# A one-core mixer kernel: means added to the transposed activations one step sooner, and query features of tiles 10 to 15 transposed by VectorE through DRAM instead of by TensorE

## The chip, the cores and the metric

The kernel runs on one core of one Trainium2 chip. The metric is the device time of one execution in microseconds (us). Three timed executions of the kernel before gave 625.36, 626.11 and 626.40 us: median 626.11 us. All arithmetic is float32; a product of two matrices is made of three passes on TensorE (high part by high part, high by low, low by high; lines 54 to 58), since TensorE takes its operands in a rounded form of float32.

## The reference

With x of shape 2048 x 512, the output is x plus two branches that both read the layer-normalised x. Cut to what matters:

```
xn = layernorm(x)
# branch A: linear attention, 32 heads of 16
q, k, v = split(xn @ wqkv)
phi(t)  = concat(softmax(t_head @ w_phi), softmax(-t_head @ w_phi))   # 32 features a head
kv = sum over rows of phi(k)^T v ;  z = sum over rows of phi(k)
A  = (phi(q) @ kv) / (phi(q) . z + 1e-6) @ wo
# branch B: gated MLP that mixes rows
zz = gelu(xn @ w_in);  z1, z2 = halves of zz (688 columns each)
B  = (z1 * (w_sp @ layernorm(z2) + b_sp)) @ w_out
out = x + A + B
```

## The kernel before

The 2048 rows are 16 tiles of 128 (numbered 0 to 15). Five stages follow each other, and TensorE (PE) runs the matrix products of all of them one after the other.

1. **Projections** (lines 485 to 518, up to about 205 us in the profile). The loop runs over steps s = 0 to 15. Each step makes the features of the keys of tile s (`proj_k`), the values of the next tile (`proj_v`), and, run a bit faster so that 16 are made in 13 steps, the query features (`proj_q`), which go unnormalised to DRAM in `e_d`, by a DMA on GpSimd's (POOL's) queue. In between stand pieces of `z1_raw`, the half z1 of branch B, whose matmuls read as `zps`.
   Tiles 6 to 15 of x come already transposed from DRAM (`lay_x`, tile `xc` or `xt`). Their row means are not subtracted on an engine: `send_mean(s+4)` computes the means of tile s+4 (VectorE; a sign change on POOL, line 311; SyncE (SP) stores them to DRAM in `nm_d`, line 312), and `center_t` issues, on POOL's queue, a DMA that reads the means from `nm_d` as a broadcast and adds them to `xc` as it lands (line 318). `split_x(s+2)` then makes the two parts of `xT` (ScalarE, line 48; VectorE, line 52), which TensorE multiplies in the next step. In step s the call was `center_t(s+3)`: the tile whose means had been sent a step before, and whose `xT` is made one step later.
   The running sum of the key features is made by accumulating DMAs on POOL's queue too (`zacc`, line 342).
2. **The second half of branch B's input** (`zproj` with `w2`, gelu, layer norm), up to about 290 us.
3. **The row mixing** w_sp @ z2 in seven products of a Strassen form (`products`, matmuls `g`), up to about 490 us.
4. **Output** (lines 1016 to 1044), up to the end. It goes over pairs of tiles i = 0, 2, ... 14. In program order TensorE does for a pair: `project_u(i)` (15 + 2 matmuls of branch B's output product), `attend` (32 small matmuls `po` of query features by kv), `project_u(i+1)`, `project_o(i)`, `project_o(i+1)` (12 matmuls each, adding branch A's output product), and then `attend_T(i+2)`: 16 transposes on TensorE (`ptq`, line 936) of the next pair's query features, which ScalarE copies to `f` (line 938). `po` of the next pair reads `f`.
   The query features come back from `e_d` (`load_q`, tile `et`, SP's queue). `features(s)`, three tiles ahead of the pair's loop, normalises them with seven VectorE instructions (`q_fin`, lines 542 to 549) and a DMA on POOL's queue copies them to a rounded tile `er` (line 905), which the transposes read. VectorE also makes the low parts of `u` and of `oT` (`ul`, `oT`, line 52), which `project_u` and `project_o` read.
   The last rows of branch B's gate are still made in this stage (`gate` at i = 8, lines 785 to 798): a VectorE transpose in blocks of 32 x 32 (line 795), four stores on SP's queue to `u_d`, and loads of `u` from there for tiles 14 and 15 (line 813). The same way of turning a tile, over DRAM in four stores of one block each, had been used for all other tiles before.
   Output tiles go out by accumulating DMAs on POOL's queue (`out<-xr`, line 984); `xr` has three buffers, the PSUM tile `out` two.

Instructions of an engine run in the order in which they stand in its program, and the DMAs of SP and of POOL are issued in that order too: one that waits holds up all behind it. That order is made from the code by a scheduler with estimated times, within the bounds that `tc.issue_after` sets. `xz_tile`/`slot` is a ring of 16 buffers shared by `et`, `qtmp` and others; a buffer is given out again when its readers are done.

Of the kernel before, what the change touches and what calls it, by code (L numbers as in the profile page):

```python
# [10 lines left out]
F32 = mybir.dt.float32  # L11
# [7 lines left out]
P = 128  # L19
S, D, H, DH, FH = 2048, 512, 32, 16, 688  # L20
NT = S // P
ND = D // P
FC = FH // 2
NG = 4
NF = 2 * D
# [3 lines left out]
BL = 32  # L29
EPS_LN = 1e-5  # L30
EPS_DEN = 1e-6
XB = 5
FT, LT = 6, 13
NP = NT // 2
HP, QP = P // 2, P // 4
FP = 3 * P
# [4 lines left out]
def mixer(ctx: ExitStack, tc: tile.TileContext, x, x_t, wv, wqkT, phi_bd, wo, w_in, wst, b_r, w_out, out):  # L41
    nc = tc.nc
    pe, act, dve, pool, sp = nc.tensor, nc.scalar, nc.vector, nc.gpsimd, nc.sync
# [34 lines left out]
    u_d = dram.tile([NT, FU, P], F32, name="u_d")  # L78
    kvT_d = dram.tile([P, D], F32, name="kvT_d")
    zb_d = dram.tile([P, NF], F32, name="zb_d")  # L80
    nm_d = dram.tile([NT, ND, P], F32, name="nm_d")

    ident = cst.tile([P, P], F32, name="ident")
# [13 lines left out]
    def heads(ap):  # L97
        return ap.rearrange("p (h d) -> p h d", d=DH)
# [8 lines left out]
    def bc(ap, n):  # L107
        return ap.unsqueeze(2).to_broadcast([P, n, DH])
# [66 lines left out]
    with ExitStack() as p0:  # L175
# [138 lines left out]

        def center_t(s):

            with tc.issue_after(send_mean.last):
                pool.dma_start(lay[s], nm_d[s].rearrange("c t -> (c t)").unsqueeze(0).to_broadcast([P, D]), accum_op=ALU.add)

        def keep_v(s, p):  # L320
# [12 lines left out]

        def proj_q(s):
            e = softmax_pair(wk, proj(s, wqk_h[:, 0], wqk_l[:, 0]), "q", r_x[:, s:s + 1])
            pool.dma_start(e_d[s], e)

        def add_kv(s, er):

# [142 lines left out]
        keep(pe=zproj.last)  # L482
        spare.update(zip((2, 3, 4, 5, 8, 9), [bd_t] + wkT_t + wqT_t[:1] + [None] * 2))
        n1, nq = 1, 0
        for s in range(NT):
            if s + 4 < FT:
                fetch(s + 4)
            if FT <= s + 6 < NT:
                fetch(s + 6)
            if FT <= s + 4 < NT:  # L490
                lay_x(s + 4)
            er = ek[s] if s < len(ek) else proj_k(s)
            if 1 < s < FT - 2:
                centered(s + 2)
            elif FT - 2 <= s < NT - 2:
                with tc.issue_after(softmax_pair.last[0]), tc.issue_after(softmax_pair.last[1]):
                    split_x(lay.pop(s + 2))
            if FT <= s + 4 < NT:
                send_mean(s + 4)
            if FT <= s + 3 < NT:  # L500
                center_t(s + 3)
            while nq < (s - 2) * NT // (NT - 3):
                proj_q(nq)
                nq += 1
            add_kv(s, er)
            if s == 0:
                tiles = fold_tiles(((za, "z"), (ps, "mm")))
                keep(pe=fold(0, wqT, tiles))
                folded(0, tiles)
            elif s == 1:  # L510
                proj_v(3)
            elif 2 < s < NT - 1:
                proj_v(s + 1)
            while n1 < s * (NT - LAG) // (NT - 1):
                z1_raw(wk, za, n1, 2)
                n1 += 1
            if s == 3:
                queue.close()
# [19 lines left out]
    def q_fin(et, tmp, zb):  # L538

        e, r, t, w = et[:, :NF], *(et[:, NF + k * 2 * H:NF + (k + 1) * 2 * H] for k in range(3))  # L540
        den = et[:, NF + 6 * H:QW]
        dve.tensor_tensor(tmp, e, zb, op=ALU.mult)
        dve.tensor_reduce(t, heads(tmp), axis=AX.X, op=ALU.add)
        dve.tensor_tensor(t, t, r, op=ALU.mult)
        dve.scalar_tensor_tensor(den, pairs(t, 0), EPS_DEN, pairs(t, 1), op0=ALU.add, op1=ALU.add)
        dve.reciprocal(den, den)
        dve.tensor_tensor(w.rearrange("p (h a) -> p h a", a=2), r.rearrange("p (h a) -> p h a", a=2),
                          den.unsqueeze(2).to_broadcast([P, H, 2]), op=ALU.mult)
        return e, dve.tensor_tensor(heads(e), heads(e), bc(w, 2 * H), op=ALU.mult).ins

    QC = 4
    NQ = NT // QC
# [249 lines left out]
    def slot(name, dt=F32):  # L802
        return xz_tile(2 * FH, dt, name)
# [92 lines left out]

    def features(s):
        with tc.issue_after(fin[-1]):
            es[s], ins = q_fin(ets.pop(s), slot("qtmp")[:, :NF], zb)
        fin.append(ins)  # L900
        if s == 3:
            return
        e = es[s]
        es[s] = cw.tile([P, NF], F32R, tag="er", bufs=6, name="er")
        lasts[6] = pool.dma_start(es[s].bitcast(F32), e).ins
# [19 lines left out]
    def attend_T(s):  # L925

        fs = []
        for g in range(NG):
            pt = pst.tile([P, 2, 2, P], F32, tag="tr", name="ptq")
            for a in range(2):  # L930
                for k in range(2):
                    src = group(es[s + k], 2 * g + a)
                    if src.dtype == F32:
                        pe.transpose(pt[:, a, k], src, ident)
                    else:
                        pe.transpose(pt[:, a, k].bitcast(F32R), src, ident_r)  # L936
            f = wk.tile([P, 2, 2 * P], F32, tag="f", bufs=NG + 1, name="f")
            lasts[5] = act.activation(f, pt.rearrange("p a k b -> p a (k b)"), AF.Copy).ins
            fs.append(f)
        return fs  # L940
# [137 lines left out]
```

## Time and profile before

| | |
|---|---|
| median of three timed runs | 626.11 us |
| the profiled execution, its time | 625.34 us |
| its span, first to last instruction | 623.6 us |
| granted TensorE clock, mean | 0.999 |
| VectorE (DVE) busy | 508.3 us (82%) |
| ScalarE (ACT) busy | 272.8 us (44%) |
| GpSimd (POOL) busy | 113.7 us (18%) |
| DMA moved | 103.67 MB, mean 166 GB/s |

The rows quoted below come from the page of the profiled execution (engines, chain of the work that ended last, DMA issues) and from answers of its trace: waits by engine, timelines by engine (start in us, length in us, engine, line, operation, output <- input, shape, and in brackets the idle time before and what ended it), and windows (busy us of each engine in a stretch, number of instructions, granted clock, DMA share, GB/s). A matmul's length there is longer than the step to the next one, since matmuls are pipelined: what counts is from start to start. For a DMA the trace shows the issue on its queue, and "us to landing" is counted from there.

### The profile page before, as it was taken

Reading aid. Unit: us, or ns where it says so; the run is one execution under the profiler, and the core shown is the slowest. Engines: PE = TensorE matmul, PEld = TensorE weight load, DVE = VectorE, ACT = ScalarE, POOL = GpSimd, SP = SyncE. Lnnn points to the kernel's source line nnn. Section 1 sums busy time; section 2 is a strip of 40 time slices with the busy share of each in tenths; the row PEclk is TensorE's granted clock in tenths of the full one; section 3 lists DMA queues with packets and bytes.
Section 4 is the critical chain, followed back from the end, with each engine's and each line's share of the span. In section 5 each row is a group of like instructions: output and inputs, shape, how many; then the busy total and the mean of one; then the engine's idle time right before and its main releaser. Section 6 shows DMA issues by size and latency. Waiting matters only on the chain.

```text
span 623.6 us, 11439 instructions
## 1 busy us (share of the span) xinstructions
PE 615.1 (99%) x4366; PEld 561.5 (90%) x4366; DVE 508.3 (82%) x903; ACT 272.8 (44%) x436; POOL 113.7 (18%) x198
## 2 busy tenths in 40 slices
PE   8999999999999999999999999999999999999997
PEld 7888888878889999999999999999999887788785
DVE  5999899899988498988989888696959899989211
ACT  4652324333433558876435433253444433334331
POOL 4122233222211025541000000000000212211110
PEclk9999999999999999999999999999999999999999
DMA  9557676566546757002464745637477799984722
GB/s 318 189 138 165 162 183 187 152 165 172 118 154 186 271 210 270 2 1 67 129 128 136 196 89 155 156 97 173 88 177 244 225 284 332 328 243 111 162 38 48
DMA packets 90671, 103.67 MB, mean 166 GB/s; under 512 B 47080, under 2 KB 60136, under 8 KB 90376
## 3 DMA queue, kind: packets, MB, share of 16 engines
q1 hardware_dynamic: 76840, 60.76, 34.0%
q0 software_dynamic: 11472, 36.54, 23.6%
q10 hardware_dynamic: 2304, 5.64, 2.4%
q8 instruction: 34, 0.56, 0.4%
q14 instruction: 21, 0.17, 0.1%
HBM read 61.61 MB, written 30.56 MB: 148 GB/s over the span
## 4 chain that ended last, share of the span: by engine, by line
PE 85%; DMA 6%; DVE 4%; issue 3%; POOL 1%; ACT 1%; DVEq 0%; POOLq 0%
PE g L58 11%; PE g L57 10%; PE g L56 10%; PE zps L58 6%; PE zps L56 6%; PE zps L57 6%; PE pout L56 5%; PE pout L58 5%; PE pout L57 5%; DMA xc<-nm_d 5%; PE proj L56 4%; PE proj L57 4%; PE proj L58 4%; PE ptq L936 1%; PE po L951 1%
## 5 line engine op out<-in xcount | busy, mean ns | idle before, releaser
L57 PE MATMUL g<-B,A 128*128 128x344 f32 x448 | 143.4, 320 | 0.0
L56 PE MATMUL g<-B,A 128*128 128x344 f32 x448 | 142.9, 320 | 0.0
L58 PE MATMUL g<-B,A 128*128 128x344 f32 x448 | 140.7, 321 | 0.1
L56 PEld LDWEIGHTS g<-B,A 128*128 128x128 f32 x448 | 84.3, 188 | 0.0
L57 PEld LDWEIGHTS g<-B,A 128*128 128x128 f32 x448 | 84.2, 188 | 0.0
L58 PEld LDWEIGHTS g<-B,A 128*128 128x128 f32 x448 | 83.7, 188 | 0.4 <-DVE A L52 0.4
L48 ACT ACTIVATE A<-S 128x512 fp32r<-128x512 f32 x64 | 39.2, 629 | 76.3 <-DVE S L588 61.3
L121 ACT ACTIVATE e<-e,r_x 128x1024 f32<-128x1024 f32 x26 | 29.9, 1150 | 56.3 <-DVE e L120 55.1
L56 PE MATMUL proj<-wqk_h,xT 128*128 128x512 f32 x128 | 50.1, 391 | 0.0
L57 PE MATMUL proj<-wqk_l,xT 128*128 128x512 f32 x128 | 50.0, 390 | 0.0
L58 PE MATMUL proj<-wqk_h,xT 128*128 128x512 f32 x128 | 49.9, 390 | 0.0
L48 ACT ACTIVATE A<-wf 128x512 fp32r<-128x512 f32 (+1 forms) x64 | 33.1, 519 | 33.3 <-DMA wf<-in_wst 12.6
L52 DVE TENSOR_TENSOR A<-S,A 128x512 fp32r<-128x512 f32 x64 | 43.0, 686 | 4.4 <-ACT A L48 4.0
L56 PE MATMUL zps<-w_0h,xT 128*128 128x344 f32 x128 | 41.1, 321 | 0.0
L56 PE MATMUL zps<-w_1h,xT 128*128 128x344 f32 x128 | 40.9, 319 | 0.0
L58 PE MATMUL zps<-w_0h,xT 128*128 128x344 f32 x128 | 40.8, 319 | 0.0
L58 PE MATMUL zps<-w_1h,xT 128*128 128x344 f32 x128 | 40.7, 319 | 0.0
L57 PE MATMUL zps<-w_1l,xT 128*128 128x344 f32 x128 | 40.6, 318 | 0.0
L57 PE MATMUL zps<-w_0l,xT 128*128 128x344 f32 x128 | 40.6, 318 | 0.0
L753 POOL DMA_DIRECT2D z1t<-z_d x16 | 8.6, 545 | 166.9 <-DMA u_d<-z1t 124.9
L52 DVE TENSOR_TENSOR A<-wf,A 128x512 fp32r<-128x512 f32 (+1 forms) x64 | 35.0, 549 | 1.8 <-ACT A L48 1.8
L124 DVE TENSOR_REDUCE sm<-e 128x64 f32<-128x1024 f32 x26 | 31.2, 1200 | 1.7 <-ACT e L121 1.5
(218 smaller groups left out, 1430.6 us busy)
## 6 DMA issues: line engine op xcount, KB each, us to landing
wf<-in_wst SPq DMA_DIRECT2D x64, 256.0 KB, 3.1
e_d<-e POOLq DMA_DIRECT2D x16, 544.0 KB, 5.0
et<-e_d SPq DMA_DIRECT2D x16, 544.0 KB, 5.2
er<-et POOLq DMA_DIRECT2D x12, 512.0 KB, 5.5
z_d<-z1f ACTq DMA_DIRECT2D x16, 344.0 KB, 2.3
z1t<-z_d POOLq DMA_DIRECT2D x16, 344.0 KB, 5.3
zacc<-e POOLq DMA_DIRECT2D x10, 512.0 KB, 4.7
u<-u_d SPq DMA_DIRECT2D x15, 320.0 KB, 6.3
```

What stands on the lines that cost most here:

```text
L48: return act.activation(h, src, AF.Copy).ins
L52: return (eng or dve).tensor_tensor(l, src, h.bitcast(F32), op=ALU.subtract).ins
L56: pe.matmul(dst, ah, bh, start=start, stop=False)
L57: pe.matmul(dst, ah, bl, start=False, stop=False)
L58: return pe.matmul(dst, al, bh, start=False, stop=stop).ins
L121: softmax_pair.last = less, act.activation(e, e, AF.Exp, scale=scale).ins
L124: dve.tensor_reduce(sm, heads(e), axis=AX.X, op=ALU.add)
L753: pool.dma_start(t[:, k, :FH], z1_d[2 * i + k])
L936: pe.transpose(pt[:, a, k].bitcast(F32R), src, ident_r)
L951: lasts[3] = pe.matmul(po[r][c * QP:(c + 1) * QP, k], kvT[rows, m // 2, cols], fs[m // 4][rows, m // 2 % 2], start=True, stop=True).ins
```

## The change

Two things are changed. First, in stage 1 step s calls `center_t(s + 4)` in place of `center_t(s + 3)`, behind `proj_q` in place of ahead of it, and the DMA is put behind the last `e_d` store in POOL's order. So the means of a tile are added in the step that sends them. Second, from tile TQ = 10 on, `features(s)` transposes the normalised features with VectorE (`turn_q`: 128 x 1024 in blocks of 32 x 32, into the tile `qtmp`), stores them in four DMAs on POOL's queue to a new DRAM tensor `q_d` in runs of 32 elements (128 bytes), and drops the copy to `er`; `attend_T` of the pairs 10, 12 and 14 is then four loads of `f` on SP's queue (`load_f`, 256 KB each, in runs of 1 KB), with no TensorE transpose and no ScalarE copy. The diff, cut:

```diff
+TQ = 10
...
+    q_d = dram.tile([NP, NF, 2, P], F32, name="q_d")
...
         def center_t(s):
-            with tc.issue_after(send_mean.last):
+            with tc.issue_after(send_mean.last), tc.issue_after(proj_q.last or send_mean.last):
                 pool.dma_start(lay[s], nm_d[s].rearrange("c t -> (c t)").unsqueeze(0).to_broadcast([P, D]), accum_op=ALU.add)
...
         def proj_q(s):
...
-            pool.dma_start(e_d[s], e)
+            proj_q.last = pool.dma_start(e_d[s], e).ins
...
             if FT <= s + 4 < NT:
                 send_mean(s + 4)
-            if FT <= s + 3 < NT:
-                center_t(s + 3)
             while nq < (s - 2) * NT // (NT - 3):
                 proj_q(nq)
                 nq += 1
+            if FT <= s + 4 < NT:
+                center_t(s + 4)
             add_kv(s, er)
...
+    def turn_q(s, dst, e, eng=sp):
+        ins = dve.transpose(dst, e).ins
+        q = q_d[s // 2, :, s % 2].rearrange("(m j) t -> j m t", j=BL)
+        for b in range(0, P, BL):
+            turn_q.last = eng.dma_start(q[:, :, b:b + BL], dst[b:b + BL].rearrange("p (m t) -> p m t", t=BL)).ins
+        return ins
+
+    def load_f(s, f, g):
+        sp.dma_start(f, q_d[s // 2, 2 * g * P:2 * (g + 1) * P].rearrange("(a p) k t -> p a (k t)", p=P))
+        return f
...
     def features(s):
         with tc.issue_after(fin[-1]):
-            es[s], ins = q_fin(ets.pop(s), slot("qtmp")[:, :NF], zb)
+            tmp = slot("qtmp")[:, :NF]
+            es[s], ins = q_fin(ets.pop(s), tmp, zb)
+            if s >= TQ:
+                ins = turn_q(s, tmp, es.pop(s), pool)
         fin.append(ins)
+        if s >= TQ:
+            return
...
     def attend_T(s):
         fs = []
+        if s >= TQ:
+            return [load_f(s, wk.tile([P, 2, 2 * P], F32, tag="f", bufs=NG + 1, name="f"), g) for g in range(NG)]
```

The lines of the new program are numbered 1 to 22 higher, so line 52 reads as 53, 318 as 320, 549 as 552, and 798 as 813. How the order moves, at three places:

On POOL, in a step of stage 1, the program before reads (`mask` holds the means that line 311 turns in sign, `xc<-nm_d` is the adding DMA of `center_t`, and the brackets name what an instruction waits for: DMAHW is a DMA of SP or ScalarE, DMASW one of POOL):

```order
L311 TENSOR_SCALAR mask<-mask 128x32 [waits DVE_49]
L94 TENSOR_SCALAR mask<-mask 128x1
L318 DMA xc<-nm_d 128x512 [waits DMAHW3_49,DMAHW0_49]
L95 TENSOR_TENSOR r_x<-mask,mhalf 128x1 [waits Pool_49]
L342 DMA zacc<-e 128x1024 [waits DMASW1_49,DMASW4_49,DVE_49,Activation_49]
L336 DMA e_d<-e 128x1088 [waits DMASW5_49,DVE_49,Activation_49]
```

and now:

```order
L313 TENSOR_SCALAR mask<-mask 128x32 [waits DVE_49]
L96 TENSOR_SCALAR mask<-mask 128x1
L97 TENSOR_TENSOR r_x<-mask,mhalf 128x1 [waits Pool_49]
L320 DMA xc<-nm_d 128x512 [waits DMAHW5_49,DMAHW4_49]
L344 DMA zacc<-e 128x1024 [waits DMASW2_49,DMASW5_49,DVE_49,Activation_49]
L338 DMA e_d<-e 128x1088 [waits DMASW6_49,DVE_49,Activation_49]
```

The place is nearly the same, between the sign change and `zacc`; the tile is another: the DMA now waits for the store of the means that the sign change just ahead of it has released.

On PE, where pair 8 ends and pair 10 begins (`woh` is the high part of wo, `wu` of w_out), the program before reads:

```order
L58 MATMUL pout<-woh,oT 128x512
L936 MATMUL ptq<-zb,er 128x128 [waits DMASW2_49,PE_49]
L936 MATMUL ptq<-zb,er 128x128 [waits DMASW3_49]
L936 MATMUL ptq<-zb,er 128x128 x2
L936 MATMUL ptq<-zb,er 128x128 [waits PE_49]
L936 MATMUL ptq<-zb,er 128x128 x3
L936 MATMUL ptq<-zb,er 128x128 [waits PE_49]
L936 MATMUL ptq<-zb,er 128x128 x3
L936 MATMUL ptq<-zb,er 128x128 [waits PE_49]
L936 MATMUL ptq<-zb,er 128x128 x3
L56 MATMUL pout<-wu,uh 128x512 [waits Activation_49]
```

and now:

```order
L57 MATMUL pout<-woh,oT 128x512
L58 MATMUL pout<-wol,oT 128x512
L59 MATMUL pout<-woh,oT 128x512
L57 MATMUL pout<-wu,uh 128x512 [waits Activation_49]
L58 MATMUL pout<-wu,uh 128x512
L59 MATMUL pout<-wu,ul 128x512
```

The 16 transposes are gone between the last matmul of `project_o(9)` and the first of `project_u(10)`, and so they are for pairs 12 and 14. Where `po` of these pairs waited for ScalarE's copy, it now waits for the loads of `f`.

On VectorE and SP in the last part of the program, VectorE before reads, from the features of tile 13 to those of 14:

```order
L549 TENSOR_TENSOR et<-et 128x1024
L542 TENSOR_TENSOR qtmp<-et,zb 128x1024
L52 TENSOR_TENSOR oT<-po,oT 128x2x256 x2
L543 TENSOR_REDUCE et<-qtmp 128x64
L52 TENSOR_TENSOR ul<-u,uh 128x640
L544 TENSOR_TENSOR et<-et 128x64
L545 SCALAR_TENSOR_TENSOR et<-et 128x32
L788 TENSOR_TENSOR z1t<-z1t,c 128x2x688
```

and now, from the same instruction on:

```order
L552 TENSOR_TENSOR et<-et 128x1024
L803 TENSOR_TENSOR z1t<-z1t,c 128x2x688
L556 STREAM_TRANSPOSE qtmp<-et 128x1024
L545 TENSOR_TENSOR qtmp<-et,zb 128x1024
L805 CAST z1t<-z1t 128x2x48
L546 TENSOR_REDUCE et<-qtmp 128x64
L53 TENSOR_TENSOR z1t<-z1t 128x2x48
L547 TENSOR_TENSOR et<-et 128x64
L810 STREAM_TRANSPOSE zt<-z1t 128x1472
```

Each of the tiles 10 to 15 has a transpose behind its last feature instruction. SP's last rows before were:

```order
L535 DMA et<-e_d 128x1088
L798 DMA u_d<-zt 32x46x32 x4
L813 DMA u<-u_d 128x5x128
L814 DMA rt<-u_d 96x128
L813 DMA u<-u_d 128x5x128
L814 DMA rt<-u_d 96x128
L973 DMA xr<-in_x 128x512
```

and are now:

```order
L538 DMA et<-e_d 128x1088 x2
L563 DMA f<-q_d 128x2x256 x4
L813 DMA u_d<-zt 32x46x32 x4
L563 DMA f<-q_d 128x2x256 x4
L828 DMA u<-u_d 128x5x128
L829 DMA rt<-u_d 96x128
L828 DMA u<-u_d 128x5x128
L829 DMA rt<-u_d 96x128
L563 DMA f<-q_d 128x2x256 x4
L995 DMA xr<-in_x 128x512
```

The loads of pair 10 stand ahead of the four stores of `u_d`, those of pair 12 behind them and ahead of the loads of `u` for tiles 14 and 15, and those of pair 14 behind these.

More of the change, by code (lines that the diff above doesn't have):

```diff
@@ L484, in mixer @@
         n1, nq = 1, 0
+        proj_q.last = None
         for s in range(NT):
```

## The prediction

> **What bounds the kernel now.** I read the engines first, then what TensorE (PE) waited for, then the two places that the change touches, and last the slack of the engines and queues that take over work.
>
> ```profile
> PE 615.1 (99%) x4366; PEld 561.5 (90%) x4366; DVE 508.3 (82%) x903; ACT 272.8 (44%) x436; POOL 113.7 (18%) x198
> PE proj L56 <- ACT xT L48: 1.2, 1, 1.2
> PE ptq L936 <- DVE c L771: 0.8, 1, 0.8
> ```
>
> The first row is the page's busy time; the others are from the view of PE's waits over the whole run (who waited for whom, us in all, times, longest), which has only one row more, at the very start. PE is busy for 99% of the span and waits three times. So time falls in two ways only: a wait of PE goes, or PE gets less to do. The change does one of each, and moves the work to engines that are not the bound. The wait for `xT` is the first part's; here it is in the timelines of PE, POOL, ScalarE and SP:
>
> ```profile
> 126.07 0.39 PE L58 MATMUL proj<-wqk_h,xT 128*128 128x512 f32 x1
> 127.68 0.50 PE L56 MATMUL proj<-wv_h,xT 128*128 128x512 f32 x1 [1.22 <-ACT xT L48]
> 121.44 0.93 POOL L318 DMA_DIRECT2D xc<-nm_d  x1
> 127.00 0.63 ACT L48 ACTIVATE xT<-xc 128x512 fp32r<-128x512 f32 x1 [2.23 <-DMA xc<-nm_d]
> 106.81 0.54 SPq L312 DMA_DIRECT2D nm_d<-mask  x1
> ACT xT L48 <- DMA xc<-nm_d: 17.0, 7, 4.0
> ```
>
> Matmuls of this shape follow each other every 0.22 to 0.23 us (the rows of the next fence); here it is 1.61 from start to start, so 1.4 us are lost. The transposed tile comes from ScalarE at 127.00, ScalarE had been free since 124.77 and waited for the adding DMA, which POOL issued at 121.44. The means that this DMA adds were stored from 106.81 on, 14.6 us earlier. The last row (waits from 50 to 140 us) says that ScalarE waits so for seven tiles, 17.0 us in all; only at this one does PE run dry.
>
> **Part 1: the means a step sooner.** It removes no instruction. The DMA of this tile can go out once its own means have landed in DRAM. The trace has no landing for that store; the nearest are other stores and loads by the hardware queues:
>
> ```profile
> z_d<-z1f ACTq DMA_DIRECT2D x16, 344.0 KB, 2.3
> xc<-in_x_t SPq DMA_DIRECT2D x7, 256.0 KB, 6.8
> xc<-nm_d POOLq DMA_DIRECT2D x7, 256.0 KB, 5.2
> 84.04 0.32 POOL L311 TENSOR_SCALAR mask<-mask 128x32 f32<-128x32 f32 x1 [2.25 <-DVE mask L310]
> 88.65 0.90 POOL L342 DMA_DIRECT2D zacc<-e  x1 [2.50 <-DVE e L341]
> 109.75 0.62 POOL L336 DMA_DIRECT2D e_d<-e  x1 [1.19 <-ACT v L322]
> ```
>
> With 2.3 to 6.8 us the means of 106.81 have landed by 109.6 to 114.2 (0.54 for the issue); the DMA follows the `e_d` store of 109.75, so it is issued by 110.4 to 114.2 and lands 5.2 later, by 115.6 to 119.4. ScalarE wants it at 124.77: at least 5 us to spare. I take the whole 1.4 us. Nothing else is late there: in the new order VectorE's part of `xT` also stands earlier in the step. PE does no less in this stage, so more than the one wait (1.4, or 1.5 with the slow first step behind it) is not to be had; the 17.0 us of ScalarE are off the path.
>
> What it costs: POOL now waits for the landing, with `zacc` and the next `e_d` behind it. The tightest step in the rows above is that at 84.04: `zacc` was issued at 88.65, and the DMA ahead of it would now wait from 84.9 to 87.2 at best and 91.7 at worst, plus 0.9, so `zacc` is 0 to 4 us late there. A late `zacc` holds back a buffer of key features that VectorE fills two steps later; PE does not wait for that in any row. I take 0, and keep 1.4 (the gain of this part) as the other end.
>
> **Part 2: 48 transposes less on PE.** Pair 10's, in PE's timeline:
>
> ```profile
> 570.54 0.39 PE L57 MATMUL pout<-wol,oT 128*128 128x512 f32 x1
> 570.76 0.39 PE L58 MATMUL pout<-woh,oT 128*128 128x512 f32 x1
> 571.00 1.50 PE L936 MATMUL ptq<-zb,er 128*128 128x128 f32 x16
> 572.33 0.46 PE L56 MATMUL pout<-wu,uh 128*128 128x512 f32 x1
> 572.63 0.39 PE L57 MATMUL pout<-wu,uh 128*128 128x512 f32 x1
> 569.60 0.60 ACT L983 ACTIVATE xr<-pout 128x512 f32<-128x512 f32 x1 [2.61 <-PE pout L58]
> 602.81 1.50 PE L936 MATMUL ptq<-zb,er 128*128 128x128 f32 x16
> 604.14 0.46 PE L56 MATMUL pout<-wu,uh 128*128 128x512 f32 x1
> ```
>
> The rows show the first and the last of the three blocks. The first matmul of the next pair starts 1.33 us after the transposes did, and its own step to the next is 0.30 instead of 0.23, which goes too: 1.33 to 1.40 us a pair, 4.0 to 4.2 for three. I take 4.1. What is late next? That matmul waits for ScalarE to empty its PSUM tile, done at 569.60 + 0.60 = 570.20, 0.8 us before it could start at 571.00; the same holds in each pair, since both move together.
>
> What takes over: VectorE turns six tiles, POOL issues 24 stores where it issued 6 copies, SP issues 12 loads, ScalarE drops 12 copies. Nothing of it is on PE's path unless `f` comes late for `po` or VectorE brings `oT` late. When `f` is needed, and when the features were ready:
>
> ```profile
> 576.46 1.02 PE po L951 x32
> 592.36 1.02 PE po L951 x32
> 608.27 1.02 PE po L951 x32
> 548.95 1.22 DVE L549 TENSOR_TENSOR et<-et 128x1024 f32<-128x1024 f32 x1
> 561.66 1.22 DVE L549 TENSOR_TENSOR et<-et 128x1024 f32<-128x1024 f32 x1
> 577.32 1.22 DVE L549 TENSOR_TENSOR et<-et 128x1024 f32<-128x1024 f32 x1
> 567.35 1.58 DVE L788 TENSOR_TENSOR z1t<-z1t,c 128x1376 f32<-128x1376 f32 x1
> 571.82 1.71 DVE L795 STREAM_TRANSPOSE zt<-z1t 128x1472 f32<-128x1472 f32 x1
> ```
>
> The chain gives the starts of `po` for pairs 10, 12 and 14; the next three rows end the features of tiles 11, 13 and 15 (550.2, 562.9, 578.5). VectorE was 26, 29 and 30 us ahead. A turn of 1024 columns is not in the trace; 1.71 us for 1472 gives 1.2 as an estimate. Six make 7.1 us. By the new order two turns stand before the end of pair 10's, four (and the 1.6 us gate product, now ahead) before the end of pair 12's, six before pair 14's; with 1 to 2 us of new waiting for ScalarE's `uh`, the turned tiles are ready at about 554.4, 570.6 and 586.8. `po` moves up by 1.4, 2.8 and 4.1 in its turn (the wait of part 1 and the earlier pairs move both sides of this sum): needed at 575.1, 589.6 and 604.2. That leaves **20.7, 19.0 and 17.4 us** for the way through DRAM. What that way takes, from the page's DMA issues:
>
> ```profile
> u_d<-z1t POOLq DMA_DIRECT2D x4, 184.0 KB, 7.4
> u_d<-zt SPq DMA_DIRECT2D x4, 184.0 KB, 4.6
> u<-u_d SPq DMA_DIRECT2D x15, 320.0 KB, 6.3
> wf<-in_wst SPq DMA_DIRECT2D x64, 256.0 KB, 3.1
> L798 POOL DMA_DIRECT2D u_d<-z1t x4: 900/910/944, 494.1 to 496.8; - x4
> 573.55 5.84 SPq L798 DMA_DIRECT2D u_d<-zt  x4
> 500.00:520.00 20.00, 20.00 (x124) 16.10 (x123) 19.48 (x30) 6.57 (x11) 2.93 (x4) 1.00 1.03 310
> 560.00:580.00 20.00, 20.00 (x152) 15.44 (x151) 18.05 (x27) 8.69 (x14) 3.38 (x5) 1.00 0.56 133
> 580.00:600.00 20.00, 20.00 (x125) 15.99 (x125) 3.77 (x5) 6.46 (x11) 1.72 (x2) 1.00 0.47 105
> ```
>
> The first rows are stores in the same 128-byte runs, on POOL and on SP, and loads of a similar size; then the issue on POOL (0.91 us each) and on SP, and three windows (busy us of PE, weight loads, VectorE, ScalarE, POOL, then clock, DMA share, GB/s). A way is: up to 0.9 for one more issue ahead on POOL, 2.7 for three issues, 4.6 to 7.4 for the fourth store to land, 3.1 to 6.3 for the first load, 1.5 to 2.5 for the other three: **12.8 to 19.8 us**. The slow ends were taken where the DMA engines were full (1.03 from 500 to 520), while the stretches in question stand at 0.56 and 0.47, so I take a value near the quick end: nothing is late, with 0 to 2.4 us (19.8 less 17.4) as the bounds of a wait for pair 14. Pair 12 has an obstacle of its own: SP issues its loads behind the four stores of `u_d`, which took from 573.55 to 579.39 and begin about 1.5 later now, so at the earliest at 580.9; 6.3 + 2.5 from there is 589.7, just at the limit.
>
> VectorE has room: of the 40 us in the last two windows it is busy for 18.05 + 3.77 = 21.8, and 7.1 more fit. In the first of these it is nearly full, so `oT` could wait behind a turn of 1.2 us; going through the new order by these durations I find `oT` of pair 10 done at 579.0. PE ends its `po` at 576.1 and has 17 matmuls of 0.23 to do before `project_o`, where the third is the first to read the low part: 580.5. No cost.
>
> **The sum.** 1.4 + 4.1 = 5.5 us less than the profiled execution: its own time is 625.34 us (span 623.6, 1.7 around it), so 619.8. The median of the runs shown is 626.11, 0.8 above that execution, so a median is to be expected at 626.1 - 5.5 = **620.6 us**.
>
> A rule of the Trainium skill (DMA: Bandwidth & Descriptors, section Specifications) speaks against the second part: transfers under 512 bytes do not run at line rate, because the DMA engine does a read-modify-write; the turned tiles are stored in 128-byte runs. The row of 184 KB in 7.4 us agrees that such stores are slow (a load of 320 KB took 6.3). But that row has the same runs, so by it the sum stays; if the read-modify-write came on top and doubled the landing, the way would be that of the last rival.
>
> **The rivals.**
> - *One way through DRAM is late.* For: the slow rows and pair 12's limit. Against: the DMA engines are half idle there. It gives back 1 to 3 us: 621.6 to 623.6.
> - *Part 1 brings nothing*, because PE's matmuls of stage 1, which the scheduler set in another order, run dry elsewhere, or `zacc` on POOL is late: 626.1 - 4.1 = 622.0. For: the chain of waits from 54 to 127 us runs through VectorE and these DMAs much of the time, so they are close to PE. Against: every `xT` is ready sooner, and PE had one wait in 150 us.
> - *No change*: both of these with a wait of 3 us or more: 625 to 626.
> - *Slower: the stores hold PE at the last pair.* Stores in 128-byte runs land in 14.8 us, twice the row of POOL. The four of tile 15 follow those of tile 14 closely, and the loads wait for the last. The way is 0.9 + 2.7 + 14.8 + 8.8 = 27.2, and PE, with nothing else to do, waits 27.2 - 17.4 = 9.8 us: 630.4. It decides from a way of 17.4 + 5.5 = 22.9 us on, where the gain is used up. Against: 22.9 is 3 us above the sum of the slowest rows.
>
> **How the numbers follow.** The forecast, both gains whole or nearly so, 619.3 to 621.6: 0.60. One way late: 0.19. Part 1 without effect: 0.08. No change: 0.05. Slower: 0.08. The range from 619.3 (all upper ends: 4.2 + 1.5, and some spread of the runs) to 623.6 takes in the first three, 0.87, with the ends of the unknown costs (2.4 and 1.4) inside it. Faster by over 0.2% (below 624.9; about what a measurement of this kernel can tell from no change) are the first three: 0.87; the same 0.05; slower 0.08.
>
> **What would show it.** Right: no wait of PE for `xT` near 127; ScalarE's 17.0 us for the adding DMAs gone; 48 matmuls less; a plain 0.23 us step from `project_o` to `project_u` at pairs 10, 12 and 14; `f` landed before `po`. Wrong: a wait of PE at `po` on `f<-q_d` (way too long), at `project_o` on `oT` (VectorE too full), or a new wait between 54 and 205 (part 1). What would make the forecast wrong most is a landing of the 128-byte stores far over 7.4 us.

## The result, and the profile after

| | before | after |
|---|---|---|
| median, five runs of each on the same chip | 625.36 us (624.79 to 626.40) | 632.86 us (632.21 to 635.17) |
| the profiled execution, its time | 625.34 us | 632.86 us |
| its span | 623.6 us | 631.2 us |
| granted TensorE clock, mean | 0.999 | 0.989 |

The ratio is 1.0117, with a 95% interval of 1.0095 to 1.0140: the change makes the kernel 1.2% slower, where the forecast was 0.9% faster. (Two of the ten executions of one kernel below, `k1`, took 859 us at a granted clock of 0.66, and the numbers given for it leave them out.) From the page of the profile after, the engines:

```profile
PE 613.3 (97%) x4318; PEld 558.2 (88%) x4318; DVE 514.5 (82%) x909; ACT 265.4 (42%) x424; POOL 129.7 (21%) x216
```

The 48 transposes are gone (4366 to 4318 matmuls), but TensorE now has 97% of the span where it had 99%. What it waited for in the whole run (us, times, longest; the rows left out are the one at the very start and two of 0.4 and 0.2 us near 7 us):

```profile
PE po L973 <- DMA f<-q_d: 10.2, 1, 10.2
PE ptq L958 <- DVE c L786: 0.3, 1, 0.3
```

There is one large wait, for `f`, and it is of the kind the prediction named. TensorE's timeline around `po` of pairs 10 and 12 shows where it is:

```profile
573.21 1.09 PE L973 MATMUL po<-f,kvT 64*32 64x256 f32 x32
574.24 0.50 PE L57 MATMUL pout<-wu,uh 128*128 128x512 f32 x1
...
587.13 0.63 PE L987 MATMUL pout<-wu,rt 96*128 96x512 f32 x2
597.91 3.11 PE L973 MATMUL po<-f,kvT 64*32 64x256 f32 x32 [10.16 <-DMA f<-q_d]
600.95 0.80 PE L57 MATMUL pout<-wu,uh 128*128 128x512 f32 x1
...
603.56 0.39 PE L57 MATMUL pout<-wu,uh 128*128 128x512 f32 x1
```

Pair 10 was not held up. At pair 12 `po` starts 10.2 us late, and what follows is slow: `po` takes 3.04 us to the next matmul in place of 1.03, and the six steps from 600.95 to 603.56 take 2.61 us where 0.33 and five of 0.23 would make 1.48. That is 10.2 + 2.0 + 1.1 = 13.3 us. With it the forecast of 619.8 us for a profiled execution becomes 633.1, against 632.86 measured: nothing else of size is missing. The slow `po` has two causes, which experiment `e1` below takes apart. The granted clock was 0.50 in the windows of the trace from 590 to 603 us. And the four loads of `f` still came one by one: `po` is four groups of eight, one for each load, and the weight loads (PEld) of the second to fourth group waited for theirs:

```profile
598.44 0.20 PEld L973 LDWEIGHTS po<-f,kvT 64*32 64x32 f32 x8 [0.33 <-DMA f<-q_d]
599.15 0.20 PEld L973 LDWEIGHTS po<-f,kvT 64*32 64x32 f32 x8 [0.51 <-DMA f<-q_d]
599.94 0.20 PEld L973 LDWEIGHTS po<-f,kvT 64*32 64x32 f32 x8 [0.59 <-DMA f<-q_d]
```

Why `f` came late is seen on SyncE's and GpSimd's queues. These are the issues of `u_d` and of pair 12's `f`, and of GpSimd's rows those of `q_d` for tiles 13 to 15:

```profile
573.24 11.26 SPq L813 DMA_DIRECT2D u_d<-zt  x4
584.86 9.40 SPq L563 DMA_DIRECT2D f<-q_d  x4
```

```profile
569.36 3.53 POOL L559 DMA_DIRECT2D q_d<-qtmp  x4
578.65 3.16 POOL L559 DMA_DIRECT2D q_d<-qtmp  x4 [4.79 <-DVE qtmp L556]
585.45 3.48 POOL L559 DMA_DIRECT2D q_d<-qtmp  x4
```

The four stores of `u_d` took 5.84 us to issue before (573.55 to 579.39) and 11.26 now, up to 584.5. The loads for pair 12 stand behind them: they go out from 584.86 to 594.26, and `po` was due at 587.7. GpSimd's stores fall into the same time. The windows (busy us of PE, weight loads, VectorE, ScalarE and GpSimd, then clock, DMA share and GB/s), and three of the rows of DMA issues from 540 to 610 us (KB each, median us to landing):

```profile
540.00:560.00 20.00, 20.00 (x152) 15.43 (x151) 18.37 (x26) 6.76 (x13) 9.21 (x12) 1.00 0.96 230
560.00:580.00 20.00, 20.00 (x115) 15.82 (x115) 19.33 (x28) 6.78 (x10) 8.66 (x11) 1.00 0.93 158
580.00:600.00 20.00, 9.84 (x63) 6.74 (x65) 4.79 (x8) 1.20 (x2) 6.79 (x9) 0.74 0.95 183
```

```profile
q_d<-qtmp POOLq DMA_DIRECT2D x24, 128.0 KB, 6.1
f<-q_d SPq DMA_DIRECT2D x12, 256.0 KB, 5.6
u_d<-zt SPq DMA_DIRECT2D x4, 184.0 KB, 15.3
```

The DMA engines, at 0.56 and 0.47 from 560 to 600 before, are at 0.93 and 0.95, and that at only 158 and 183 GB/s: they are full without moving much. The one store of `u_d` whose landing the trace has took 15.3 us to land; before, the one took 4.6. The page's rows for the queues of SyncE (q1) and GpSimd (q0) show the price over the whole run (packets, MB, share of 16 engines' span), first before:

```profile
q1 hardware_dynamic: 76840, 60.76, 34.0%
q0 software_dynamic: 11472, 36.54, 23.6%
```

and after:

```profile
q1 hardware_dynamic: 80104, 63.91, 35.0%
q0 software_dynamic: 11760, 36.54, 25.8%
```

On GpSimd's queue the bytes are the same (24 stores of 128 KB take the place of 6 copies of 512 KB), but it kept the engines busy for 25.8% of 631.2 = 162.8 us in place of 23.6% of 623.6 = 147.2 us, 15.6 us more. SyncE's has the loads of `f` besides, 35.0% of 631.2 less 34.0% of 623.6, 8.9 us more.

### The profile page after: what moved, and what is told of

Its sections match the earlier page's. It is cut to its first block, busy times and chain, and to the rows that moved or that the text cites. A ratio compares the mean times of both kernels' runs of the same rounds, so it can differ in the third digit from the quotient of the medians.

```text
span 631.2 us, 11366 instructions
## 1 busy us (share of the span) xinstructions
PE 613.3 (97%) x4318; PEld 558.2 (88%) x4318; DVE 514.5 (82%) x909; ACT 265.4 (42%) x424; POOL 129.7 (21%) x216
## 3 DMA queue, kind: packets, MB, share of 16 engines
q0 software_dynamic: 11760, 36.54, 25.8%
q10 hardware_dynamic: 2304, 5.64, 2.3%
## 4 chain that ended last, share of the span: by engine, by line
PE 92%; DMA 3%; DVE 2%; SPq 2%; issue 1%; ACT 0%; DVEq 0%
PE g L59 11%; PE g L58 11%; PE g L57 11%; PE proj L58 7%; PE proj L57 7%; PE proj L59 7%; PE zps L59 6%; PE zps L57 6%; PE zps L58 6%; PE pout L57 4%; PE pout L58 4%; PE pout L59 4%; DMA f<-q_d 2%; SPq L813 2%; PE po L973 1%; PE kvps L355 1%
## 5 line engine op out<-in xcount | busy, mean ns | idle before, releaser
L49 ACT ACTIVATE A<-wf 128x512 fp32r<-128x512 f32 (+1 forms) x64 | 32.8, 518 | 29.8 <-DMA wf<-in_wst 15.1
```

The source lines that it names most:

```text
L49: return act.activation(h, src, AF.Copy).ins
```

## The experiments

Fourteen kernels ran. The theory from this profile was: the loads of pair 12 are late because `u_d`'s stores stand ahead of them, and those are slow because of `q_d`'s. The rivals were: part 1 costs something; only the order on SyncE's queue matters; the bytes are too many in any form. Ratios are to the kernel before on the same chip, with 95% intervals.

### The two parts apart

Part 1 alone is the changed kernel with `TQ = 16`:

```diff
-TQ = 10
+TQ = 16
```

> Part 1 alone: the means are added a step sooner, no tile is turned through DRAM (TQ = 16). Theory 'late f' (all of the loss is the wait of TensorE for the f loads of pair 12 and what follows it): the stall of 1.4 us at 126 to 127.7 us is gone and nothing else changes, so 1.4 us less than the kernel before, 624.0 us, ratio 0.998. Rival 'means' (part 1 costs something in stage 1 or 2 that the whole change hides): 625.4 us or more.

It took 624.50 us, ratio 0.9974 (0.9956 to 0.9991). TensorE has no wait for `xT` left. Part 1 brings what was forecast for it (1.4 of 625.8 us is 0.9978).

Part 2 alone has `center_t(s + 3)` at its old place:

> Part 2 alone: the six tiles are turned through DRAM, center_t stands as before. Theory 'late f': the same wait at pair 12 with everything 1.4 us later, 634.3 us. Rival 'means': 632.9 us or less.

It took 633.97 us, ratio 1.0129 (1.0113 to 1.0144), with the wait for `xT` back and the same wait of 10 us for `f`. So the loss is all in part 2.

### Is it the order?

Three kernels move the same bytes in another order. In the first, `u_d`'s four stores go on GpSimd's queue, so nothing stands ahead of `f`:

```diff
-                (pool if i == NP - 2 else sp).dma_start(dst[:, :, b:b + BL], src[b:b + BL].rearrange("p (m b) -> p m b", b=BL))
+                (pool if i >= NP - 2 else sp).dma_start(dst[:, :, b:b + BL], src[b:b + BL].rearrange("p (m b) -> p m b", b=BL))
```

> The whole change, but the four stores u_d<-zt are issued on GpSimd's queue, so that the f loads of pair 12 stand on SyncE's queue behind no store. All bytes and runs are the same. Theory 'order': the loads go out once the stores of tile 13 (issued from 569.4, landing in up to 10 us) have landed, at 577 to 583, and land 4 to 9 us later, at 581 to 590, where po of pair 12 is due at 587.6: a wait of 0 to 2.5 us, 619.4 to 622 us in all. Rival 'bytes' (the 128-byte stores fill the DMA engines whatever the order, so the loads get no share before about 595): 630 to 633 us.

It took 633.32 us, ratio 1.0127 (1.0090 to 1.0164). TensorE's timeline at pair 12:

```profile
590.22 0.64 PE L973 MATMUL po<-f,kvT 64*32 64x256 f32 x8 [2.03 <-DMA f<-q_d]
592.22 1.08 PE L973 MATMUL po<-f,kvT 64*32 64x256 f32 x8 [1.37 <-DMA f<-q_d]
595.68 1.08 PE L973 MATMUL po<-f,kvT 64*32 64x256 f32 x8 [2.37 <-DMA f<-q_d]
597.26 1.08 PE L973 MATMUL po<-f,kvT 64*32 64x256 f32 x8 [0.51 <-DMA f<-q_d]
```

The loads went out from 579.1 to 584.4, 6 to 10 us sooner, and still came one by one up to 597: the last had a landing of 14.3 us. TensorE's four waits add up to 6.3 us, in place of one of 10.2, and the kernel is no faster. So standing behind `u_d` is at most a part of what makes the loads late; the theory that the order alone does it falls, and the rival's range was nearly met.

In the second, `u_d`'s stores (and the loads of `u` that need them) stand behind the loads for pair 12:

```diff
...
+        if i == 10:
+            with tc.issue_after(load_f.last):
+                store_u()
+            p2.close()
+            for s in (14, 15):
+                us[s] = fetch_u(s)
```

> The whole change, but the stores u_d<-zt stand behind the f loads of pair 12 on SyncE's queue (and the loads of u for tiles 14 and 15 behind them). All bytes and runs the same. Theory 'DMA time' (between 570 and 604 us the DMA engines have 31 us of work in 34 us; what stands last in the order waits): f12 is issued when tile 13's stores have landed, at about 578, and lands by 583 to 588; u_d then goes from 580 to about 592, u lands by 598 to 600, where project_u(14) wants it at about 600: waits of 0 to 3 us in all, 620.6 to 624 us. Rival (the engines are too full in any order): the wait only moves from f12 to u of tile 14 or f14 and stays near 8 us or more, 629 us or more.

It took 633.59 us, ratio 1.0112 (1.0078 to 1.0145): my number was too low, the rival's held. The wait of TensorE and the issue of `u_d`:

```profile
PE pout L57 <- ACT oT L49: 11.9, 1, 11.9
```

```profile
579.94 14.67 SPq L818 DMA_DIRECT2D u_d<-zt  x4
599.66 0.38 SPq L833 DMA_DIRECT2D u<-u_d  x1
```

`f` is in time, `u_d` takes 14.67 us, `u` of tile 14 is loaded only from 599.66 on, and ScalarE, whose `uh` of that tile stands ahead of `oT`, holds TensorE for 11.9 us. In the third, the gate and with it `u_d` come one pair sooner:

```diff
-    GATE_LAST = 8
+    GATE_LAST = 6
```

> The whole change with the last gate two tiles pairs' loop steps earlier (GATE_LAST 6 in place of 8), so that the four stores of u_d go out some 14 us sooner, between tile 11's and tile 12's stores, and nothing stands ahead of f of pair 12 but f of pair 10. All bytes and runs the same. Theory 'DMA time, last in order waits': of the 57 us of DMA work from 540 to 600 some 11 us (stores of tiles 14 and 15, loads of u for 14 and 15) can come behind f12, so 46 us are to be done in the 47.6 us up to 587.6: f12 lands with 0 to 4 us of waiting, and f of pair 10 may be up to 3 us late too: 621 to 627 us. Rival 'order' (f12 is late only for standing behind u_d): no wait at all, 619.8 to 621 us.

It took 633.27 us, ratio 1.0107 (1.0064 to 1.0149), and both my numbers were wrong: now pair 10 is hit.

```profile
PE po L973 <- DMA f<-q_d: 12.7, 1, 12.7
```

```profile
557.32 10.39 SPq L813 DMA_DIRECT2D u_d<-zt  x4
...
581.31 1.92 SPq L563 DMA_DIRECT2D f<-q_d  x4
```

`u_d` meets the stores of tiles 11 and 12 and again takes 10 us. Here the order does the rest: the load of `u` for tile 14 now stands ahead of `f` of pair 10, waits for `u_d`'s landing and goes out at 577.83, so that `f` goes out only at 581.31. In each order something is late, and TensorE waits 6 to 13 us for it.

### Is it the number of tiles?

With tiles 10 to 13 alone turned (`s >= TQ` becomes `s in TURNED`):

```diff
-TQ = 10
+TURNED = (10, 11, 12, 13)
```

> The whole change with tiles 10 to 13 alone turned (14 and 15 as before). Theory 'DMA time': tile 13's stores still meet u_d, but those of tiles 14 and 15 (8 of 24, issued from 578.7 on) don't, so f of pair 12 lands some 4 to 8 us sooner: a wait of 2 to 6 us with 0 to 2 us for the clock, so 624 to 629 us. Rival 'order' (the f loads are late only because they stand behind u_d): a wait near 8 us or more, 630 us or more.

It took 629.92 us, ratio 1.0060 (1.0042 to 1.0077), just above the range. `u_d`'s issue took 9.93 us, and `f` was waited for for 5.7 us: without the stores of tiles 14 and 15 the loads come sooner, and tiles 12 and 13 are enough to slow `u_d`. With `TURNED = (10, 11, 14, 15)`:

> The whole change with tiles 10, 11, 14 and 15 turned, 12 and 13 as before. No load of f stands behind u_d, and f of pair 14 is not due before about 604. Both theories: no wait for f; 1.4 us for the means and 2 x 1.37 us for the transposes off the kernel before, 621.2 to 622 us, ratio 0.993 to 0.995. If there is a wait of more than 2 us all the same, the stores of tiles 14 and 15 alone slow u_d and the loads of u for tile 14.

It took 621.42 us (620.69 to 622.56), ratio 0.9922 (0.9897 to 0.9947): **faster than both kernels**, and close to what the sum of the prediction gives for two pairs. TensorE waits for no `f`, and SyncE's row for `u_d` is nearly that of before:

```profile
571.06 5.78 SPq L813 DMA_DIRECT2D u_d<-zt  x4
```

A try to add pair 8, `TURNED = (8, 9, 10, 11, 14, 15)`:

> A try at a faster version: tiles 8, 9, 10, 11, 14 and 15 turned, 12 and 13 as before. If VectorE (95 percent busy from 540 to 580) and the DMA engines (0.9 and more) have room for two more tiles ahead of pair 10: 1.37 us less than without tiles 8 and 9, 620.0 us. If not (f of pair 8 or 10 late, or oT): waits of 1 to 4 us, 621 to 624 us.

It took 625.06 us (619.55 to 628.63), ratio 0.9982 (0.9954 to 1.0009). In the profiled execution, at 628.58 us, TensorE waits four times for `f` of pair 8, 5.0 us in all. The best run reached the 620.0 us hoped for, the median did not: the stretch ahead of 560 us has no room to spare either (the DMA share from 540 to 560 was 1.00).

### What in the stores costs so much?

`h1` keeps number, bytes, queues and packets of the stores, and makes their runs 4 KB long:

```diff
-        q = q_d[s // 2, :, s % 2].rearrange("(m j) t -> j m t", j=BL)
+        q = q_d[s // 2].rearrange("(p a) k t -> p (a k t)", p=P)[:, s % 2 * NF:(s % 2 + 1) * NF]
         for b in range(0, P, BL):
-            turn_q.last = eng.dma_start(q[:, :, b:b + BL], dst[b:b + BL].rearrange("p (m t) -> p m t", t=BL)).ins
+            turn_q.last = eng.dma_start(q[b:b + BL], dst[b:b + BL]).ins
```

> The whole change, but each store of q_d puts its 32 rows of 4 KB down as they are, in runs of 4 KB in place of 128 bytes; number of stores, bytes, queues and order are the same. The loads of f then read the features in another order, so branch A of tiles 10 to 15 is not computed. Theory 'runs' (the 128-byte runs make the stores keep the DMA engines busy for two to three times their bytes' time, which slows u_d and the loads of f): issue of u_d back near 6 us, f of pair 12 landed by about 587, wait of TensorE 0 to 1 us, 620 to 621.5 us. Rival 'bytes' (3.1 MB of stores and 3.1 MB of loads more than there is room for): the wait stays above 5 us, 627 us or more.

It leaves out branch A of tiles 10 to 15, which reads wrongly ordered features. It took 623.87 us (622.00 to 628.45), ratio 0.9967 (0.9945 to 0.9990), some 2 us above the range of the theory "runs" and 3 below that of "bytes". In the profiled execution `f` was waited for for 1.0 us, and `oT` for 0.7. Its rows of SyncE, and of GpSimd's queue on the page:

```profile
573.64 6.88 SPq L813 DMA_DIRECT2D u_d<-zt  x4
580.69 3.87 SPq L563 DMA_DIRECT2D f<-q_d  x3
```

```profile
q0 software_dynamic: 11760, 36.54, 24.2%
```

Packets and bytes are those of the changed kernel, and the queue kept the engines busy for 24.2% of 621.0 = 150.3 us, 3.1 more than before instead of 15.6. One thing besides the runs differs: each load of `f` here needs one store of a tile, not all four, and one of pair 12's loads came ahead of `u_d`. So the next two kernels, `s1` (short runs) and `s2` (long ones), have no load at all: part 1 with the turns and stores, while nothing reads `q_d`, and `er` and TensorE's transposes stay.

```diff
             if s >= TQ:
-                ins = turn_q(s, tmp, es.pop(s), pool)
+                ins = turn_q(s, tmp, es[s], pool)
         fin.append(ins)
-        if s >= TQ:
-            return
...
-        if s >= TQ:
-            return [load_f(s, wk.tile([P, 2, 2 * P], F32, tag="f", bufs=NG + 1, name="f"), g) for g in range(NG)]
```

> The price of the stores by themselves: part 1, and tiles 10 to 15 are turned and stored to q_d in 128-byte runs, but nothing reads q_d; the copies er and TensorE's transposes stay as before. TensorE has nothing new to wait for. Both theories: about 624.5 us, as with part 1 alone, up to 2 us more if er copies come late. Theory 'runs': from 540 to 615 us the DMA engines work some 24 us more than with part 1 alone (58 percent of 75 us), 1.0 us of all 16 engines for each of the 24 stores of 128 KB, and the issue of u_d's four stores takes 9 us or more in place of 5.8. Rival 'bytes': some 15 us more, 0.6 us a store, u_d near 6 us (its delay in the changed kernel came from the loads of f).

> The same with each store's rows put down in runs of 4 KB; nothing reads q_d. About 624.5 us. Theory 'runs': some 15 us more DMA work than with part 1 alone (0.6 us a store), u_d's issue near 6 us. Rival 'bytes': the same DMA work as with the 128-byte runs.

One execution each, so the times have the scatter of single ones (the kernel before took 623.73 to 629.88 us over all its executions): 636.37 us with the short runs, 625.96 us with the long ones (before, beside them, 625.38). With the short runs, GpSimd's queue on the page, TensorE's wait and SyncE's `u_d`:

```profile
q0 software_dynamic: 12624, 39.69, 26.6%
```

```profile
PE pout L57 <- ACT oT L49: 10.2, 1, 10.2
```

```profile
572.82 12.96 SPq L813 DMA_DIRECT2D u_d<-zt  x4
```

and with the long ones, GpSimd's queue and `u_d`:

```profile
q0 software_dynamic: 12624, 39.69, 24.9%
```

```profile
574.59 5.02 SPq L813 DMA_DIRECT2D u_d<-zt  x4
```

Part 1 alone had 23.7% of 622.8 = 147.6 us in this queue. With the 24 stores it is 26.6% of 634.6 = 168.8 us, or 24.9% of 624.2 = 155.4 us: **0.88 us of all 16 engines for a store of 128 KB in runs of 128 bytes, 0.33 us in runs of 4 KB** (to some 0.03, since the shares are given to a tenth of a per cent). I had expected 1.0 and 0.6; the direction holds, the sizes were too high. I had not expected 636 us: the stores alone, with nothing that reads them, cost 10 us, because `u` of tile 14 comes late (the chain of its work runs over the landing of `u_d`, 18.8 us, to `uh`, `oT` and `pout`). The rival "bytes" falls. The short runs also lie scattered in `q_d`, 1 KB or more from one to the next, where the long ones lie in a piece; no kernel here parts the length of a run from that.

`k1` puts the stores on SyncE's hardware queue (`turn_q(s, tmp, es.pop(s), sp)`):

> The whole change with the 24 stores of q_d on SyncE's hardware queue in place of GpSimd's software queue; same bytes, same 128-byte runs. Theory 'runs' (it is the run length that costs, whichever queue): DMA share from 550 to 590 stays at 0.9 or more and TensorE waits 5 us or more for f, u or et: 627 us or more. Rival 'software queue' (only GpSimd's queue pays so much for such runs): DMA share from 550 to 590 falls to about 0.75, waits of 0 to 3 us, 620 to 624 us.

The ratio is 1.0044 (1.0011 to 1.0078), with eight executions from 625.54 to 632.75 us. The DMA share from 550 to 590 was 0.92 in the mean, as the theory "runs" had it. In the profiled execution, the quickest, TensorE waited only 2.7 us for `f`, and `u_d` took 4.41 us to issue. SyncE's queue on the page:

```profile
q1 hardware_dynamic: 105064, 67.06, 38.7%
```

That is 241.4 us of 623.8, 20.5 more than the 220.9 of the changed kernel: 0.85 us for each of the 24 stores. So short runs cost the engines as much on either queue, and the rival "software queue" falls as to the price. TensorE all the same waits less than the 5 us or more of the theory; the experiment doesn't settle why, nor how the two queues share an engine.

Last, whether `u_d` is hit only because its own runs are of 128 bytes:

```diff
+            rows = u_d[2 * i:2 * i + 2].rearrange("k f t -> (k f t)").rearrange("(p w) -> p w", p=P)
             for b in range(0, P, BL):
+                if i == NP - 1:
+                    sp.dma_start(rows[b:b + BL], src[b:b + BL])
+                    continue
```

> The whole change, with the 128-byte runs of q_d kept, but the four stores u_d<-zt put their rows down in runs of 5.9 KB, so u of tiles 14 and 15 is read in another order and branch B of these two tiles is not computed. (On SyncE's queue the loads of u for tile 14 now stand ahead of two of the f loads of pair 12, and those of tile 15 behind them.) Theory 'two short streams' (what takes so long is u_d's 128-byte runs on one queue against q_d's on the other): u_d is issued in 3 us or less and has landed by about 580, f of pair 12 lands by 587 to 590, a wait of 0 to 2.5 us: 620 to 623 us. Rival 'q_d alone' (q_d's stores fill the engines for whatever stands on SyncE's queue): f of pair 12 lands at 592 or later, a wait of 4 us or more: 626 us or more.

It leaves out branch B of tiles 14 and 15. It took 632.22 us, ratio 1.0089 (1.0058 to 1.0120), and the wait for `f` is still there:

```profile
PE po L977 <- DMA f<-q_d: 8.1, 3, 7.1
```

`u_d` itself does well (issued in 5.64 us, landing 4.9 us), but the first load for pair 12, issued at 584.24, landed at 594.85. `q_d`'s stores hold up whatever else wants the engines then; that the loads of `u` for tile 14 stood ahead of two of these loads makes the size uncertain, not the direction.

### The slow rows behind the wait

Is it the clock, or the pieces of `f`? `e1` fills the wait with 40 matmuls whose result nobody reads:

```diff
+NPAD = 40
...
+        if i == 12:
+            with tc.issue_after(lasts[2]):
+                pad = pst.tile([P, D], F32, tag="tr", name="pad")
+                for _ in range(NPAD):
+                    lasts[2] = pe.matmul(pad, wu[0][0][:, :P], wu[0][0], start=True, stop=True).ins
```

> The whole change with 40 matmuls of 128x512 without use put on TensorE ahead of po of pair 12 (9.2 us at 0.23 us each), so that it isn't idle while it waits for f. They write a PSUM tile that nothing reads. Theory 'clock' (about 3 us of the loss come from the clock that falls while TensorE is idle: po of pair 12 at 3.1 us instead of 1.02 and the matmuls behind it at up to 0.43 us instead of 0.23): about 629.7 us, po at 1.02 us. Rival (the slow rows have another cause, such as f slices that arrive one by one): 632.9 us, po still near 3 us.

```profile
575.01 1.09 PE L974 MATMUL po<-f,kvT 64*32 64x256 f32 x32
...
589.39 9.27 PE L1048 MATMUL pad<-wu 128*128 128x512 f32 x40
598.84 1.35 PE L974 MATMUL po<-f,kvT 64*32 64x256 f32 x16 [0.17 <-DMA f<-q_d]
...
601.74 0.50 PE L58 MATMUL pout<-wu,uh 128*128 128x512 f32 x1
602.07 0.39 PE L59 MATMUL pout<-wu,uh 128*128 128x512 f32 x1
...
615.18 1.09 PE L974 MATMUL po<-f,kvT 64*32 64x256 f32 x32
```

```profile
599.55 0.15 PEld L974 LDWEIGHTS po<-f,kvT 64*32 64x32 f32 x8 [0.56 <-DMA f<-q_d]
600.39 0.16 PEld L974 LDWEIGHTS po<-f,kvT 64*32 64x32 f32 x8 [0.69 <-DMA f<-q_d]
601.17 0.16 PEld L974 LDWEIGHTS po<-f,kvT 64*32 64x32 f32 x8 [0.62 <-DMA f<-q_d]
```

The granted clock stayed at 0.999 in the mean, and the matmuls behind `po` run at their usual step, as the theory "clock" had it. But `po` of pair 12 still takes 2.90 us (598.84 to 601.74), as the rival had it: at the full clock too its groups wait for the loads of `f`, one by one. So most of `po`'s 2.0 us come from the pieces of `f`, and the 1.1 us behind it from the clock. From `po` of pair 12 to that of pair 14 it is 16.34 us (598.84 to 615.18), where the changed kernel took 17.63 (597.91 to 615.54): some 1.3 us of the loss went with the clock. (From `po` of pair 10 on it is 2.2 us less, but 0.9 of that is `f`, which came that much sooner after it: 23.83 us against 24.70.) The whole kernel did not gain them (632.62 us, ratio 1.0116, the rival's number and not the theory's): `po` of pair 10 already stands 1.8 us later than in the changed kernel. New waits for VectorE at 506 and 518 us (0.9 and 0.4 us), far from the edit, explain most of that but not all.

## Why the prediction was wrong

- **Part 1** was right: alone it gives a ratio of 0.9974, the wait for `xT` is gone, and ScalarE has no more waits for the adding DMAs.
- **The transposes** were right: `po` of pair 10 starts at 573.21 where it stood at 576.39, 3.2 us sooner, against 2.8 forecast. Of this 1.74 were there at pair 8 (560.48 to 558.74), with 0.5 from a shorter wait of `ptq` near 490 us (0.8 to 0.3), which was not forecast; 1.44 is the pair's own, for 1.37. Without pair 12 the sum holds to within a microsecond (`d2`).
- **VectorE** was right: no wait for `oT`, and the turns took 1.24 us for an estimate of 1.2.
- **The way through DRAM** is the step that failed, at pair 12. The prediction named the obstacle ("SP issues its loads behind the four stores of `u_d`") and gave the loads 580.9 us at the earliest, "just at the limit". It then took the quick end of the landings, because "the stretches in question stand at 0.56 and 0.47". That share was the kernel's before, without the change's own transfers. They took, over the run, 15.6 us more of all 16 engines on GpSimd's queue and 8.9 us more on SyncE's. From 560 to 600 us 0.44 + 0.53 of 20 us each, 19.4 us, were free; the windows after have 0.37 + 0.48 of 20 us each more, 17.0 us, so hardly any room was left. Two terms that were taken over from the kernel before were too small by this. `u_d`'s issue took 11.26 us in place of 5.84, and the loads, from the first issue to the last piece of `f` (584.86 to 599.94), 15.1 us in place of 6.3 + 2.5 = 8.8. That is 5.4 + 6.3 = 11.7 us, and TensorE lost 10.2 + 2.0 = 12.2 there. The cause is that `q_d`'s stores lay their bytes down in short, scattered runs: with long ones `u_d` took 6.88 us and TensorE waited 1.0 us for `f` (`h1`), and the stores alone, with no load behind them, hold TensorE for 10.2 us with short runs and make no wait of that kind with long ones (`s1`, `s2`).
- **The bound of the wait**, 0 to 2.4 us, was too narrow for the same reason, and it stood at pair 14, where nothing was waited for: one of its loads landed at 605.55, and `po`, which the wait at pair 12 had put off, came at 615.54. (The lower end of the way, 12.8 us, should have been 11.9, as the 0.9 of an issue ahead was "up to"; nothing rests on it.)
- **The rival "slower"** came nearest in time, 630.4 us, by luck: it had the right stores and the wrong way for them to cost. It let those of tile 15 land in 14.8 us and hold up their own loads at the last pair. `q_d`'s stores landed in 6.1 us in the median, and those of tile 15 in 8.7 to 10.0, over the 7.4 assumed at most but far from 14.8. The damage is done to others, `u_d` and the loads behind it; in `s1` nobody reads the stores, and they cost as much.
- **What stands behind a wait** was not priced: the pieces of `f` that come one by one, and the clock. The clock cost some 1.3 us (by `e1`) after a wait of 10.2 us. In `s1`, where full-size matmuls follow a wait of 10.2 us at once, 13 of them take 5.60 us where some 3.1 would be usual: 2.5 us.

The rule of the Trainium skill (DMA: Bandwidth & Descriptors, section Specifications) that transfers under 512 bytes miss the line rate was weighed and set aside, as the row of the slow landing was said to hold it already. `s1` and `s2` agree with it as to the rate, 0.88 against 0.33 us for the same bytes. What the short runs take away is the engines' time, which other transfers then lack, and the landing time of one such store doesn't show that.

## What to carry to other kernels

Before transfers are called hidden, add up what they take of the DMA engines and set it against what is free in that stretch; the share of a profile without them is only the first half of this. A share that is high at few GB/s (0.56 at 133 GB/s before, where 1.03 went with 310 earlier) is a sign that the transfers there are dear. And where a change is all gain on the bound engine, it pays to apply it only where its transfers have room: pairs 10 and 14 alone brought 0.8%, pairs 10 and 12 alone lost 0.6%, and all three lost 1.2%.

## What was not expected of the hardware

- Stores in 128-byte runs cost the engines 2.7 times those in 4 KB runs at the same number of packets and bytes. If the engine reads before it writes, the page's count doesn't show it: it has 61.61 MB of HBM reads with the short runs, the long ones, and in the kernel before.
- An issue on SyncE's queue is no fixed cost: the same four stores of `u_d` took from 4.4 to 14.7 us to issue, and all behind them waited.
- After 10.2 us without work (`s1`) TensorE ran its matmuls at 0.43 us a step from 605.55 on, without another wait, and was back at 0.23 at 611.15, 5.6 us later; in `c2`, after 11.9 us, it took 4.9 us (604.42 to 609.28). The Trainium skill (TensorE: Matmul & The Clock Gate, Part 1) has such a half rate after idling; it gives some 3.4 us of sustained work until the full rate is back, and here it was longer.
